# Six query weight blocks of 120 rows in place of five of 128, and another opening, in a one-core attention and gated-MLP kernel

## The chip, the cores and the metric

The kernel runs on one core of a Trainium2 chip. A core has five engines with queues of their own: TensorE (PE in the profile, with its weight loads as PEld), VectorE (DVE), ScalarE (ACT), GpSimd (POOL) and SyncE (SP), which here only issues DMA transfers. TensorE reads SBUF and writes PSUM (eight banks of 512 fp32 columns by 128 partitions), from which DVE or ACT copy results back to SBUF. The metric is the device time of one execution in microseconds, as the median of several runs.

## The reference

All tensors are bf16. With S = 2048 rows of x, width D = 640, H = 32 heads of 20 columns and F = 1536:

```python
xn = layernorm(x)                              # over the 640 columns, no scale or bias
q, k, v = split(xn @ wqkv)                     # wqkv: 640 x 1920, 32 heads of 20
pq, pk = q_h @ w_phi[h], k_h @ w_phi[h]        # w_phi: 32 matrices of 20 x 20
phi_q = [softmax(pq), softmax(-pq)]            # 40 features a head
phi_k = [softmax(pk), softmax(-pk)]
kv, z = sum_s phi_k^T v, sum_s phi_k           # linear attention, not causal
o   = (phi_q @ kv) / (phi_q . z + 1e-6)
out = x + o @ wo + (silu(xn @ w1) * (xn @ w3)) @ w2
```

The head matrices w_phi act on the projected q and k. The kernel folds them into the weights: with a block diagonal of the 32 matrices, xn @ (Wq @ diag(w_phi)) gives pq at once, and the same for k.

## The kernel before, in words

The rows are handled as 16 tiles of 128 rows (t = 0 to 15), the width as DC = 5 chunks of 128 columns, the MLP as four blocks of 512 rows by 12 chunks of 128 of F.

The kernel does not write its instructions in order by hand. Each part of the work is a stream, a generator of steps (`norms`, `transposes`, `fold_k`, `attention`, `loads`, `mlps` and others, from line 735 on). A planner at the end of the function picks, again and again, the step that can start first by its own costs, and appends its instructions to the engines' lists; the dictionary `done` carries conditions between streams. The order on each engine, the bank of each product and the semaphores follow from that, once, when the kernel is built. All instructions pass through one helper, so the profile gives nearly all of them line 102 (line 114 for DMA issues), and groups are told apart by their tiles.

The opening (`first_loads` at line 414, `consts` at 434, `norms` at 735, `transposes` at 798):

- Tile 0 of x is loaded in two halves, one issued by SP and one by ACT. Then SP issues tile 1, tile 2, half of V's weights (`wv`), tile 3, the first third of w1 and w3 (`w_s` in the profile), w_phi (`phi_s`), K's weights transposed by the DMA (the second half of `wqkT`), x tiles 4 to 15 in three loads, and Q's weights transposed (the first half of `wqkT`). ACT issues the other half of `wv`.
- Tile 0's statistics are made on DVE (`bn_stats` of two halves, `bn_aggr`), with the power -1/2 on POOL and the normalisation on DVE (`ln_apply`). Tile 1's are made on ACT by two sums. Tiles 2 and 3 use DVE again; the two halves of their statistics are separate steps, and tile 2's second half waits until tile 0 has been transposed.
- TensorE multiplies zeros at first (`warm_up`), transposes tile 0 against an identity (five transposes), multiplies zeros eight times more (`IDLE2`, written `PS<-t 128x128`), and then the V products of tile 0 start (`PS<-wv,xnT`), once the transposed tile has been copied from PSUM to `xnT`. `PARTS` at line 516 says in which pieces and by which engine: tile 0 in two, three chunks on ACT and two on DVE.
- The four tiles' V products, two MLP groups and four folds of K's weights come next, then the K and V products of the 16 tiles in turn (`Wkp` and `wv`). Tiles 4 to 15 are normalised on ACT or DVE and transposed by DMAs on SP (`xnT<-x_tok`, DMA_TRANSPOSE).

The folds (`block_diag` at 528, `fold_mm` at 536): `BDc` holds the block diagonal by chunks of 128 rows. Since 128 is no multiple of 20, the chunks share heads: each touches seven heads (140 columns) or eight (160 columns, split in two products of 80 at the bank's border). So a fold of one chunk of 128 input rows is six products, of 140, 140, 80, 80, 140 and 140 columns, all of 128 rows. K's five folds run early; Q's five stand behind tiles 9 to 13 in `attention`, one each, and are copied to `Wqp` by ACT or DVE.

Later stages: the sums over all tiles (`kv_sum`), then per tile the Q projection (`Wqp`), exponentials on ACT, sums and ratios on DVE and POOL, a DMA transpose (`eqT<-eq`), the token product (`KVc,eqT`), and between them the MLP groups of ten products of 512 columns; last the output products.

Of the kernel before, what the change touches and what calls it, by code (L numbers as in the profile page):

```python
# [3 lines left out]
ACT = mybir.ActivationFunctionType  # L4
# [5 lines left out]
D = 640  # L10
H = 32
DH = 20
# [237 lines left out]
def bass_parallel_sum__linear_kernel_hedgehog__glu_gated_swiglu__prompt_kernel(  # L250
# [11 lines left out]
    bf = DT.bfloat16  # L262
    LAG = 4.0
    QLEAD = 2
    IDLE1, IDLE2 = 7, 8
    f32 = DT.float32
    P = _Program(nc)

# [18 lines left out]
    GM = new("GM", [128, DC, H], bf)  # L287
    phi_s = new("phi_s", [128, DC, DH], bf)
    BDc = new("BDc", [128, DC, 8 * DH], bf)
    bst = new("bst", [128, T, 12], f32)  # L290
    mv = new("mv", [128, T, 2], f32)
    rstd = new("rstd", [128, T, 2], f32)
# [25 lines left out]

    RE = region(T * 2 * D * 2 + 96)
    ekt = new("ekt", [128, T * 2 * D + 48], bf, RE)  # L320
    hT3 = new("hT3", [128, FC, 512], bf, RE)
    w2_s = new("w2_s", [128, FC, D], bf, RE + 12288)
    eq = [new(f"eq{i}", [128, NG * 128], bf, (RKV, RE + 27648)[i // 2] + 2816 * (i % 2)) for i in range(4)]
# [5 lines left out]
    oT = new("oT", [128, DC, S], bf, RV)  # L329

    RW = region(12800)
    wqkT = new("wqkT", [128, 2 * DC, D], bf, RW)
    KVc = new("KVc", [128, NG * 64], bf, RW)
    half = new("half", [128, 2, 660], f32, RW + 1408)
    Sq = new("Sq", [128, 4, 72], f32, RW + 6688)
# [55 lines left out]
    def memset(eng, o, v):  # L391
        P.op(eng, "memset", [o], [], (o, v), cost=0.15 + free(o) / 960)
# [8 lines left out]
    out_t = out.rearrange("b (t p) d -> p (b t) d", p=128)  # L401
    wqkv_t = A_wqkv.rearrange("(c p) n -> p c n", p=128)
    phi_t = A_w_phi.rearrange("h d f -> (h d) f").rearrange("(c p) f -> p c f", p=128)
    w1_t = B_w1.rearrange("(c p) f -> p c f", p=128)
    w3_t = B_w3.rearrange("(c p) f -> p c f", p=128)

# [4 lines left out]
    def load_x(a, b):  # L411
        P.dma("SP", x_tok[:, a:b, :], x_t[:, a:b, :])

    def first_loads():
        def half_wv(eng, a):
            P.dma(eng, wv[:, :, a:a + 320], wqkv_t[:, :, 2 * D + a:2 * D + a + 320])

        P.dma("SP", x_tok[:, 0, 0:320], x_t[:, 0, 0:320])
        P.dma("ACT", x_tok[:, 0, 320:D], x_t[:, 0, 320:D])
        load_x(1, 2)  # L420
        load_x(2, 3)
        half_wv("ACT", 0)
        half_wv("SP", 320)
        load_x(3, 4)
        w13(0, 512)
        P.dma("SP", phi_s[:], phi_t)
        P.dma("SP", wqkT[:, DC:2 * DC, :], A_wqkv[:, D:2 * D], True)
        load_x(4, 8)
        load_x(8, 12)
        load_x(12, 16)  # L430
        P.dma("SP", wqkT[:, 0:DC, :], A_wqkv[:, 0:D], True)


    def consts():
        memset("DVE", t1[:, 2, :], 0.0)
        memset("DVE", warm[:], 0.0)
        act(warm[:], warm[:], ACT.Exp)
        memset("POOL", ident[:], 0.0)
        select(ident[:], 0, [[-1, 128]], 1, ALU.not_equal, 1.0)
        memset("POOL", GM[:], 1.0)  # L440
        select(GM[:], 0, [[128, DC], [-DH, H]], 1, ALU.is_ge, 0.0)
        select(GM[:], DH, [[-128, DC], [DH, H]], -1, ALU.is_gt, 0.0)
        memset("POOL", mhalf[:], -0.5)
        memset("DVE", v_heads(v2[:].rearrange("p t n -> p (t n)"))[:, :, :, DH], 1.0)
        memset("POOL", M3[:, 0:3], 1.0)
        select(M3[:, 0:3], 0, [[-40, 3]], 1, ALU.is_ge, 0.0)
        select(M3[:, 0:3], 40, [[40, 3]], -1, ALU.is_gt, 0.0)
        memset("POOL", ekt[:, T * 2 * D:T * 2 * D + 48], 1.0)
# [61 lines left out]
    def idle(n, cols):  # L510
        z = t1[:, 2, :]
        for i in range(n):
            j = 7 - i if cols == 512 else 7
            mm(bank(j, cols), z[:, 0:128], z[:, 0:cols], True, True, cost=cols / 1200)

    PARTS = (((0, 0, 3, "ACT"), (1, 3, DC, "DVE")), ((0, 0, 3, "ACT"), (1, 3, DC, "ACT")),
             ((0, 0, 3, "ACT"), (1, 3, DC, "ACT")), ((0, 0, 2, "DVE"), (1, 2, DC, "ACT")))

    def xn_transpose(t, k):
# [13 lines left out]
               phi_s[:, c, :].unsqueeze(1).to_broadcast([128, n, DH]),  # L533
               GM[:, c, h0:h1 + 1].unsqueeze(2).to_broadcast([128, n, DH]), ALU.mult)

    def fold_mm(which, dc, k, eng=None):
        first = [True, True]
        for e in range(DC):
            h0, h1 = heads_of_chunk(e)
            lo, hi = DH * h0, DH * (h1 + 1)  # L540
            for q in range(2):
                a, b = max(lo, 320 * q), min(hi, 320 * q + 320)
                if a < b:
                    mm(bank(k + q, b - a, a - 320 * q), wqkT[:, which * DC + e, 128 * dc:128 * dc + 128],
                       BDc[:, e, a - lo:b - lo], first[q], e == DC - 1 or (q == 0 and e == 2), True)
                    first[q] = False
        dst = (Wqp, Wkp)[which]
        o = dst[:, dc, :].rearrange("p (b c) -> p b c", c=320)
        if eng:
            copy(eng, o, bank2(k, 320))  # L550
        else:
            evac(o, bank2(k, 320))
# [128 lines left out]
    def mlp(b, fc, k, cut=DC, dc=None):  # L681
        n = nmlp[0] % 3
        nmlp[0] += 1
        for w, kk in ((w1_s, k), (w3_s, k + 1)):
            for i in range(DC):
                if kk > k and i == cut:
                    held.add(k // 2)
                    fold_mm(1, dc, banks(2), "ACT")
# [44 lines left out]
    done = dict.fromkeys(("w", "ln", "t", "f", "k", "n", "kv", "v", "u", "qp", "qn", "qd", "q", "o", "h", "v0", "bd"), 0)  # L733

    def norms():
        yield lambda: (first_loads(), consts())
        yield lambda: act_sum(1, ACT.Copy, bst[:, 1, 0:1])
        yield lambda: (ln_half(0, 0), ln_half(0, 1), ln_rstd(0, 1))
        yield lambda: scalar_op(1, mv[:, 1, 0:1], bst[:, 1, 0:1], -1.0 / D, 0.0)
        yield lambda: act_sum(1, ACT.Square, mv[:, 1, 1:2], mv[:, 1, 0:1])  # L740
        yield lambda: ln_apply(0)
        done["ln"] = 1
        yield lambda: ln_half(2, 0)
        yield lambda: act_rstd(1)
        while done["t"] < 1:
            yield None
        yield lambda: ln_half(2, 1)
        yield lambda: ln_apply(1)
        done["ln"] = 2
        yield lambda: ln_rstd(2, 1)  # L750
        yield lambda: ln_half(3, 0)
        yield lambda: ln_apply(2)
        done["ln"] = 3
        yield lambda: (ln_half(3, 1), ln_rstd(3, 1))
        yield lambda: ln_apply(3)
        done["ln"] = 4
        yield block_diag
        done["bd"] = 1
        todo = []
        for t in range(4, T + 2, 2):  # L760
            if t == T or t > done["k"] + 8:
                for u in todo:
                    yield lambda u=u: ln_apply(u)
                    done["ln"] = u + 1
                todo = []
            if t == T:
                break
            while t > done["k"] + 8:
                yield None
            yield lambda t=t: ln_stats(t, 2)  # L770
            for u in todo:
                yield lambda u=u: ln_apply(u)
                done["ln"] = u + 1
            todo = [t, t + 1]

    def fold_k():
        while done["u"] < 2:
            yield None
        for dc in range(1, DC - 1):
            yield lambda dc=dc: fold_mm(1, dc, banks(2), "ACT")  # L780
        done["f"] = 1

    done["w"] = 4
# [8 lines left out]
    def transposed(t):  # L792
        while done["ln"] <= t:
            yield None
        yield lambda: xn_transpose(t, banks(2))
        done["t"] = t + 1

    def transposes():
# [7 lines left out]
    def loads():  # L806
        while done["t"] < 4:
            yield None
        for t in range(4, T):
            while done["ln"] <= t:  # L810
                yield None
            yield lambda t=t: P.dma("SP", xnT[:, :, t * 128:(t + 1) * 128], x_tok[:, t, :], True)
            done["t"] = t + 1
            if t == 7:
                yield lambda: w13(512, 1024)
                done["w"] = 8
        yield lambda: w13(1024, 1536)
        done["w"] = 12

    def attention():  # L820
# [20 lines left out]
        for t in range(T):  # L841
            while done["t"] <= t:
                yield None
            yield lambda t=t: k_tile(t, banks(2))
            done["k"] = t + 1
            if t >= 4:
                yield v(t)
            if 9 <= t < 14:
                yield lambda dc=t - 9: fold_mm(0, dc, banks(2))
        yield lambda: P.dma("SP", wo_s[:], A_wo.rearrange("(c p) d -> p c d", p=128))  # L850
        done["v"] = 1

# [189 lines left out]
```

## Time and profile before

| | us |
|---|---|
| median of 3 runs | 268.14 (268.13 to 268.24) |
| the profiled execution's own time | 268.08 |
| its span, first to last instruction | 266.4 |
| TensorE busy in the span | 262.2 (98%) |
| DVE, ACT, POOL busy | 168.7, 100.8, 100.7 |
| mean granted TensorE clock | 1.000 |

The page gives one profiled execution. Its parts are the engines' busy time, the span in 40 slices, the DMA queues, the chain of waits that ended last, the costliest groups of instructions and the DMA issues. The chain is followed back from the last instruction: 96% of it is TensorE, 2% the DMA of x. In timelines a row is a group of like instructions: start, length over all of them, engine, operation, tiles, count, and in brackets the idle time before it with what ended it. Matmul lengths overlap, so the spacing of starts tells the pace. A DMA is shown by its issue (`SPq`, `ACTq`); its landing stands in the DMA view, as time from the issue.

### The profile page before, as it was taken

The page shows a single profiled execution, that of the slowest core. Times are in us where ns is not written, and L with a number is a line of the kernel's source. Part 1 is how long each engine was busy: PE and PEld are TensorE (multiplying, and loading weights), DVE is VectorE, ACT ScalarE, POOL GpSimd, SP SyncE. Part 2 cuts the span into 40 slices and gives each one's busy share as a digit, 9 for nine tenths or more (in the row PEclk, how much of TensorE's full clock was granted, in tenths as well). Part 3 has the DMA queues.
Part 4 walks back from the last instruction along what each step waited for, and adds up shares of the span by engine and source line. Part 5 has one row for each costly group of instructions (what it writes and reads, how often), then busy time and mean ns, then how long its engine had stood idle before and what let it go on. Part 6 is the DMA issues. An engine that isn't in the chain of part 4 may idle for free.

```text
span 266.4 us, 4813 instructions
## 1 busy us (share of the span) xinstructions
PE 262.2 (98%) x1959; PEld 159.4 (60%) x1959; DVE 168.7 (63%) x290; ACT 100.8 (38%) x199; POOL 100.7 (38%) x143
## 2 busy tenths in 40 slices
PE   7999999999999999999999999999999999999996
PEld 3656777777655555555554445544577777777773
DVE  4559998998766898888889877888511121212112
ACT  5667999887326334434433343322100000000000
POOL 4404896999984444455534334420000000000000
PEclk9999999999999999999999999999999999999999
DMA  7998792850393244454444444213212212131201
GB/s 211 304 320 159 145 218 53 186 190 2 100 282 75 55 92 92 86 97 81 79 81 79 80 81 79 51 35 75 49 52 75 74 59 91 52 98 49 90 36 49
DMA packets 63510, 27.73 MB, mean 104 GB/s; under 512 B 49920, under 2 KB 63488, under 8 KB 63488
## 3 DMA queue, kind: packets, MB, share of 16 engines
q1 hardware_dynamic: 62544, 26.90, 43.0%
q10 hardware_dynamic: 944, 0.52, 0.7%
q8 instruction: 15, 0.25, 0.4%
q14 instruction: 7, 0.06, 0.1%
HBM read 12.81 MB, written 2.62 MB: 58 GB/s over the span
## 4 chain that ended last, share of the span: by engine, by line
PE 96%; DMA 2%; DVE 1%; SPq 0%; POOL 0%; issue 0%
PE PS L102 96%; DMA x_tok<-in_A_x_dram 2%; SPq L114 0%; POOL rstd L102 0%; DVE bst L102 0%; DVE x_tok L102 0%; DVE xres L102 0%; DVE rstd L102 0%
## 5 line engine op out<-in xcount | busy, mean ns | idle before, releaser
L102 PE MATMUL PS<-xnT,w_s 128*128 128x512 bf16 x480 | 107.4, 379 | 0.0
L102 PEld LDWEIGHTS PS<-xnT,w_s 128*128 128x128 bf16 x480 | 45.9, 98 | 51.3
L102 PE MATMUL PS<-w_s,hT 128*128 128x320 bf16 (+2 forms) x384 | 54.9, 299 | 0.0
L102 DVE TENSOR_TENSOR xres<-PS,xres 128x640 bf16<-128x640 f32 (+2 forms) x17 | 13.4, 785 | 59.8 <-PE PS L102 59.8
L102 ACT ACTIVATE th<-PS 128x512 f32<-128x512 f32 x48 | 29.1, 605 | 48.0 <-PE PS L102 48.0
L102 PEld LDWEIGHTS PS<-w_s,hT 128*128 128x128 bf16 x384 | 37.1, 98 | 15.1
L102 DVE SCALAR_TENSOR_TENSOR t<-th,PS 128x512 bf16<-128x512 f32 x48 | 32.5, 677 | 20.2 <-ACT th L102 19.3
L102 POOL TENSOR_TENSOR ekt<-ekt,rS 128x640 bf16<-128x640 bf16 x32 | 39.6, 1277 | 2.6 <-DVE rS L102 2.6
L102 DVE SCALAR_TENSOR_TENSOR hT<-t,PS 128x512 bf16<-128x512 bf16 x48 | 33.0, 688 | 5.0
L102 ACT ACTIVATE eq<-PS 128x600 bf16<-128x600 f32 (+1 forms) x72 | 23.9, 418 | 32.0 <-PE PS L102 32.0
L102 PE MATMUL PS<-wo_s,oT 128*128 128x320 bf16 (+2 forms) x160 | 24.5, 299 | 0.0
L102 PE MATMUL PS<-wv,xnT 128*128 128x320 bf16 x160 | 24.4, 299 | 0.1
L102 PE MATMUL PS<-Wqp,xnT 128*128 128x512 bf16 (+1 forms) x160 | 24.3, 299 | 0.0
L102 PE MATMUL PS<-Wkp,xnT 128*128 128x320 bf16 x160 | 23.7, 299 | 0.0
L102 POOL TENSOR_TENSOR eq<-eq,rq 128x600 bf16<-128x600 bf16 (+1 forms) x32 | 22.7, 729 | 1.3
L102 POOL TENSOR_TENSOR rq<-rq,Sq 128x32 f32<-128x32 f32 x16 | 4.1, 255 | 50.1 <-DVE rq L102 50.1
L102 DVE TENSOR_REDUCE S<-ekt 128x64 f32<-128x1280 bf16 x16 | 22.9, 1431 | 0.0
L102 POOL TENSOR_TENSOR half<-eq 128x660 f32<-128x660 bf16 x15 | 20.4, 1358 | 4.5 <-ACT eq L102 4.5
L102 ACT ACTIVATE ekt<-PS 128x640 bf16<-128x640 f32 x32 | 20.9, 733 | 2.5 <-PE PS L102 2.5
L102 PEld LDWEIGHTS PS<-wo_s,oT 128*128 128x128 bf16 x160 | 15.5, 98 | 6.5
L102 PEld LDWEIGHTS PS<-wv,xnT 128*128 128x128 bf16 x160 | 15.4, 98 | 6.1 <-ACT xnT L102 0.2
L102 PEld LDWEIGHTS PS<-Wkp,xnT 128*128 128x128 bf16 x160 | 15.5, 98 | 5.9
(56 smaller groups left out, 178.3 us busy)
## 6 DMA issues: line engine op xcount, KB each, us to landing
w_s<-in_B_w_dram SPq DMA_DIRECT2D x6, 640.0 KB, 6.4
xres<-in_A_x_dram SPq DMA_DIRECT2D x16, 160.0 KB, 2.3
out_dram<-xres SPq DMA_DIRECT2D x15, 160.0 KB, 1.8
x_tok<-in_A_x_dram SPq DMA_DIRECT2D x3, 640.0 KB, 6.4
w_s<-in_B_w_dram SPq DMA_DIRECT2D x1, 1920.0 KB, 9.4
wo_s<-in_A_wo_dram SPq DMA_DIRECT2D x1, 800.0 KB, 7.2
x_tok<-in_A_x_dram SPq DMA_DIRECT2D x3, 160.0 KB, 4.0
wv<-in_A_wqkv_dram ACTq DMA_DIRECT2D x1, 400.0 KB, 4.0
```

What stands on the lines that cost most here:

```text
L102: o = _Op(eng, lambda: m(*args, **kw), r, w, cost)
```

## The change

Loads: tile 1 becomes ACT's first transfer, and both halves of tile 0 go out on SP, the second as SP's second issue. K's transposed weights have a tile of their own (`wkT`), placed in memory that is used later for `ekt`. Q's weights come as six blocks: block g holds the 128 columns from 120g on, transposed, of which 120 rows (six whole heads) are used; the last has 40. Three blocks are loaded where the one load stood, three behind tile 11's transposes. w_phi is loaded a second time in blocks of 120 rows (`phi_6`, two DMAs behind K's weights).

Fold: `BD6`, 120 rows by 6 blocks of 120 columns, is built on POOL by one multiplication with a mask `GM6` (three operations on POOL in `consts`), after the first MLP group. A fold of Q (`fold_q`) is five products of 120 columns and one of 40, on contiguous PSUM columns from 32 on, copied in one piece. K's fold keeps its form.

Opening: tile 0 is copied in three pieces, all on ACT (two, two and one chunk), each in a PSUM bank of its own. The zero products behind its transposes are five, not eight. The halves of tile 2's and 3's statistics are one step each; tile 2's no longer waits for tile 0's transposes and stands ahead of tile 1's normalisation on DVE. The memset of ones in v moves from DVE's start to behind the transposes of tile 3.

What follows from the planner, seen in the order of each engine: tile 3's transposes stand three products later; tile 3's V products come behind the first MLP group (ten products) instead of ahead of it. Between there and the Q projections the order is the same but for the folds. In the later stages, Q tiles 4 to 9 come in pairs (projection, MLP group, projection, token product, two groups, token product, group) where they came singly before; the numbers of products of each kind are the same.

```diff
-    IDLE1, IDLE2 = 7, 8
+    IDLE1, IDLE2 = 7, 5
...
+    GM6 = new("GM6", [128, 6], bf)
+    phi_6 = new("phi_6", [128, 6, DH], bf)
...
+    wkT = new("wkT", [128, DC, D], bf, RE + 20480)
...
-    wqkT = new("wqkT", [128, 2 * DC, D], bf, RW)
+    wqT = new("wqT", [128, 6, D], bf, RW)
+    BD6 = new("BD6", [128, 6, 120], bf, RW + 7680)
...
+        memset("POOL", phi_6[:, 5, :], 0.0)
         P.dma("SP", x_tok[:, 0, 0:320], x_t[:, 0, 0:320])
-        P.dma("ACT", x_tok[:, 0, 320:D], x_t[:, 0, 320:D])
-        load_x(1, 2)
+        P.dma("ACT", x_tok[:, 1, :], x_t[:, 1, :])
+        P.dma("SP", x_tok[:, 0, 320:D], x_t[:, 0, 320:D])
         load_x(2, 3)
...
-        P.dma("SP", wqkT[:, DC:2 * DC, :], A_wqkv[:, D:2 * D], True)
+        P.dma("SP", wkT[:], A_wqkv[:, D:2 * D], True)
+        P.dma("SP", phi_6[0:120, 0:5, :], phi_r[0:600, :].rearrange("(c p) f -> p c f", p=120))
+        P.dma("SP", phi_6[0:40, 5, :], phi_r[600:D, :])
         load_x(4, 8)
         load_x(8, 12)
         load_x(12, 16)
-        P.dma("SP", wqkT[:, 0:DC, :], A_wqkv[:, 0:D], True)
+        load_wqT(0, 3)
+
+    def load_wqT(a, b):
+        for g in range(a, b):
+            P.dma("SP", wqT[:, g, :], A_wqkv[:, 120 * g:120 * g + 128], True)
...
-        memset("DVE", v_heads(v2[:].rearrange("p t n -> p (t n)"))[:, :, :, DH], 1.0)
+        memset("POOL", GM6[:], 1.0)
+        select(GM6[:], 0, [[-DH, 6]], 1, ALU.is_ge, 0.0)
+        select(GM6[:], DH, [[DH, 6]], -1, ALU.is_gt, 0.0)
...
-    PARTS = (((0, 0, 3, "ACT"), (1, 3, DC, "DVE")), ((0, 0, 3, "ACT"), (1, 3, DC, "ACT")),
+    PARTS = (((0, 0, 2, "ACT"), (1, 2, 4, "ACT"), (2, 4, DC, "ACT")), ((0, 0, 3, "ACT"), (1, 3, DC, "ACT")),
...
+    def block_diag6():
+        o = BD6[0:120].rearrange("p c (h f) -> p c h f", f=DH)
+        tt("POOL", o, phi_6[0:120].unsqueeze(2).to_broadcast([120, 6, 6, DH]),
+           GM6[0:120].unsqueeze(1).unsqueeze(3).to_broadcast([120, 6, 6, DH]), ALU.mult)
+
+    def fold_q(dc, k):
+        c0 = k * 512 + 32
+        for g in range(6):
+            n = 120 if g < 5 else 40
+            mm(PS[:, c0 + 120 * g:c0 + 120 * g + n], wqT[0:120, g, 128 * dc:128 * dc + 128],
+               BD6[0:120, g, 0:n], g in (0, 4), g in (3, 5), True)
+        evac(Wqp[:, dc, :], PS[:, c0:c0 + D])
...
-        yield lambda: ln_half(2, 0)
         yield lambda: act_rstd(1)
-        while done["t"] < 1:
-            yield None
-        yield lambda: ln_half(2, 1)
+        yield lambda: (ln_half(2, 0), ln_half(2, 1))
         yield lambda: ln_apply(1)
...
-        yield lambda: ln_half(3, 0)
         yield lambda: ln_apply(2)
         done["ln"] = 3
-        yield lambda: (ln_half(3, 1), ln_rstd(3, 1))
+        yield lambda: (ln_half(3, 0), ln_half(3, 1), ln_rstd(3, 1))
         yield lambda: ln_apply(3)
         done["ln"] = 4
+        while done["t"] < 4:
+            yield None
+        yield lambda: memset("DVE", v_heads(v2[:].rearrange("p t n -> p (t n)"))[:, :, :, DH], 1.0)
         yield block_diag
         done["bd"] = 1
+        while done["u"] < 1:
+            yield None
+        yield block_diag6
...
-        yield lambda: xn_transpose(t, banks(2))
+        yield lambda: xn_transpose(t, banks(2 if t else 4))
...
+            if t == 11:
+                yield lambda: load_wqT(3, 6)
+                done["wq"] = 1
...
             if 9 <= t < 14:
-                yield lambda dc=t - 9: fold_mm(0, dc, banks(2))
+                while not done["wq"]:
+                    yield None
+                yield lambda dc=t - 9: fold_q(dc, banks(2))
```

More of the change, by code (lines that the diff above doesn't have):

```diff
@@ L403, in bass_parallel_sum__linear_kernel_hedgehog__glu_gated_swiglu__prompt_kernel @@
     phi_t = A_w_phi.rearrange("h d f -> (h d) f").rearrange("(c p) f -> p c f", p=128)
+    phi_r = A_w_phi.rearrange("h d f -> (h d) f")
     w1_t = B_w1.rearrange("(c p) f -> p c f", p=128)
@@ L534, in block_diag, with fold_mm @@
                GM[:, c, h0:h1 + 1].unsqueeze(2).to_broadcast([128, n, DH]), ALU.mult)
-    def fold_mm(which, dc, k, eng=None):
+    def block_diag6():
[9 more added lines that the diff above has]
+        evac(Wqp[:, dc, :], PS[:, c0:c0 + D])
+    def fold_mm(dc, k, eng=None):
         first = [True, True]
@@ L543, in fold_mm @@
                 if a < b:
-                    mm(bank(k + q, b - a, a - 320 * q), wqkT[:, which * DC + e, 128 * dc:128 * dc + 128],
+                    mm(bank(k + q, b - a, a - 320 * q), wkT[:, e, 128 * dc:128 * dc + 128],
                        BDc[:, e, a - lo:b - lo], first[q], e == DC - 1 or (q == 0 and e == 2), True)
                     first[q] = False
-        dst = (Wqp, Wkp)[which]
-        o = dst[:, dc, :].rearrange("p (b c) -> p b c", c=320)
+        o = Wkp[:, dc, :].rearrange("p (b c) -> p b c", c=320)
         if eng:
@@ L687, in mlp @@
                     held.add(k // 2)
-                    fold_mm(1, dc, banks(2), "ACT")
+                    fold_mm(dc, banks(2), "ACT")
                     held.discard(k // 2)
@@ L731, in banks @@
         return min((k for k in range(0, 8, n) if k // 2 not in held), key=free_at)
-    done = dict.fromkeys(("w", "ln", "t", "f", "k", "n", "kv", "v", "u", "qp", "qn", "qd", "q", "o", "h", "v0", "bd"), 0)
+    done = dict.fromkeys(("w", "ln", "t", "f", "k", "n", "kv", "v", "u", "qp", "qn", "qd", "q", "o", "h", "v0", "bd", "wq"), 0)
     def norms():
@@ L779, in fold_k @@
         for dc in range(1, DC - 1):
-            yield lambda dc=dc: fold_mm(1, dc, banks(2), "ACT")
+            yield lambda dc=dc: fold_mm(dc, banks(2), "ACT")
         done["f"] = 1
```

## The prediction

> **What bounds the kernel now.** I read the page first, then the chain of waits, then the busy time by stage, then the opening as a timeline. The first row is the page's part 1; the others are stages, each with its length, then busy time of PE, its weight loads, DVE, ACT and POOL; then the longest piece of the chain.
>
> ```profile
> PE 262.2 (98%) x1959; PEld 159.4 (60%) x1959; DVE 168.7 (63%) x290; ACT 100.8 (38%) x199; POOL 100.7 (38%) x143
> ...
> 7.56:13.25 5.69, 5.69 (x50) 4.07 (x51) 2.66 (x9) 4.09 (x8) 2.37 (x6) 1.00 1.21 299
> 13.25:62.00 48.75, 48.75 (x375) 33.70 (x373) 44.03 (x74) 42.28 (x66) 34.56 (x47) 1.00 0.76 174
> 62.00:184.00 122.00, 122.00 (x935) 63.66 (x933) 99.10 (x168) 48.99 (x116) 60.51 (x76) 1.00 0.42 87
> ```
>
> ```profile
> 7.56 256.48 PE PS L102 x1926
> ```
>
> From 7.56 us, where TensorE transposes tile 1, the chain is TensorE alone, and each stage has it busy for its whole length. So the change pays in two places only: what starts that run earlier, and TensorE time removed from it. Anything that makes it wait is a loss in full.
>
> The opening, from the timeline (start, length, engine, operation):
>
> ```profile
> 0.80 0.41 ACTq L114 DMA_DIRECT2D x_tok<-in_A_x_dram  x1
> 0.81 1.34 SPq L114 DMA_DIRECT2D x_tok<-in_A_x_dram  x3
> ...
> 3.07 0.50 DVE L102 MEMSET v<- 128x528 bf16 x1 [1.85 <-issue]
> ...
> 3.19 0.82 DVE L102 BATCH_NORM_STATS2 bst<-x_tok 128x6 f32<-128x320 bf16 x2
> ...
> 4.22 0.74 ACT L102 ACTIVATE t<-x_tok 128x640 bf16<-128x640 bf16 x1 [0.99 <-DMA x_tok<-in_A_x_dram]
> ...
> 4.54 0.57 POOL L102 TENSOR_TENSOR rstd<-rstd,mhalf 128x1 f32<-128x1 f32 x1 [1.28 <-DVE rstd L102]
> ...
> 5.16 0.44 DVE L102 TENSOR_SCALAR x_tok<-x_tok,mv,rstd 128x640 bf16<-128x640 bf16 x1
> ...
> 5.65 0.45 PE L102 MATMUL PS<-ident,x_tok 128*128 128x128 bf16 x5 [0.38 <-DVE x_tok L102]
> ...
> 5.94 0.61 PE L102 MATMUL PS<-t 128*128 128x128 bf16 x8
> ...
> 6.10 0.47 ACT L102 ACTIVATE xnT<-PS 128x384 bf16<-128x384 bf16 x1
> ...
> 6.63 0.85 PE L102 MATMUL PS<-wv,xnT 128*128 128x320 bf16 x5
> ...
> 7.94 0.77 ACT L102 ACTIVATE xnT<-PS 128x384 bf16<-128x384 bf16 x2 [1.37 <-PE PS L102]
> ...
> 10.92 0.45 PE L102 MATMUL PS<-ident,x_tok 128*128 128x128 bf16 x5
> ...
> 11.21 2.20 PE L102 MATMUL PS<-wv,xnT 128*128 128x320 bf16 x15
> 11.25 0.29 DVE L102 COPY xnT<-PS 128x256 bf16<-128x256 bf16 x1 [0.38 <-PE PS L102]
> ...
> 13.25 4.05 PE L102 MATMUL PS<-xnT,w_s 128*128 128x512 bf16 x18
> ```
>
> Tile 0's statistics end at 4.01; call this E. Its transposes start 1.64 later (5.65), its first product after 0.98 more (6.63), and tile 1's transposes at 7.56, which is E+3.55. The eight idle products fill TensorE while tile 0 is copied; products follow each other at 0.136 (fifteen between 11.21 and 13.25), so the five of 6.63 have issued by 7.31 and TensorE then waits 0.25 for tile 1, whose sum on ACT began only at 4.22.
>
> **The change part by part.** *Loads of tiles 0 and 1.* Landing times, from the DMA view of short stretches (last number: us from issue):
>
> ```profile
> x_tok<-in_A_x_dram SPq DMA_DIRECT2D x1, 160.0 KB, 2.9
> x_tok<-in_A_x_dram ACTq DMA_DIRECT2D x1, 80.0 KB, 2.5
> x_tok<-in_A_x_dram SPq DMA_DIRECT2D x1, 80.0 KB, 2.3
> ```
>
> Tile 0's halves land at 3.1 and 3.3, tile 1 (SP's second issue, 1.26) at 4.2. Afterwards tile 1 goes out at 0.80 on ACT, tile 0's second half as SP's second issue, about 0.81+0.41 = 1.22. Its landing L is not in the trace. Early bound: the quickest half, 1.22+2.3 = 3.5. Late bound: now 240 KB stand ahead of it, and with it 320 KB, as many as had to land when tile 1 did at 4.2. I take 3.75, nearer the early row, since it is half a tile, issued like that row and beside a tile whose transfer starts at 0.80. Statistics of one half take 0.47, so E = 3.75+0.02+0.47 = 4.24, 0.23 later than now.
>
> [...]
>
> *Three copies, five idle products.* Tile 3's first copy starts 0.33 after its transposes. A 256-column copy on ACT takes about 0.38 (the pair of 384 and 256 columns takes 0.77, the first alone 0.47, with some overlap), so tile 0's first product starts 0.33+0.38+0.05 = 0.76 after its transposes instead of 0.98. The other two copies follow about 0.28 apart and hold the third and fifth product by hundredths: five products end 1.45 after the transposes, at E+1.64+1.45 = E+3.09. The idle products end 0.57 after, before the copy. DVE: tile 1's rstd follows tile 0's apply (E+1.6), then both halves of tile 2's statistics (0.86) and tile 1's apply at E+2.45, so tile 1 is ready at E+2.95. TensorE is the later one, and the 0.25 wait goes. Tile 1's transposes: 4.24+3.09 = 7.33, that is -0.23 (between -0.48 for L=3.5 and +0.22 for L=4.2).
>
> *From there on* the same 35 products and 15 transposes follow. Tile 3's last ten products move behind the first MLP group, which needs tile 3's copy: transposes +0.33+0.29+0.05 = 0.67 against 0.56 of cover (five transposes, two products), a new wait of 0.1; today's gaps in this stretch (5.69 against 35x0.136+15x0.058 = 5.63) are worth 0.06 and go. Net +0.05.
>
> ```profile
> w_s<-in_B_w_dram SPq DMA_DIRECT2D x1, 640.0 KB, 6.5
> ...
> wqkT<-in_A_wqkv_dram SPq DMA_TRANSPOSE x1, 10.3
> ...
> 11.97 1.97 POOL L102 TENSOR_TENSOR BDc<-phi_s,GM 128x140 bf16<-128x140 bf16 x5 [1.59 <-DMA phi_s<-in_A_w_phi_dram]
> ...
> 14.28 7.76 SPq L114 DMA_TRANSPOSE wqkT<-in_A_wqkv_dram  x1
> ...
> 17.14 0.48 PE L102 MATMUL PS<-BDc,wqkT 128*128 128x140 bf16 x6
> ...
> 20.71 0.23 POOL L102 TENSOR_SCALAR rstd<-mv 128x2 f32<-128x2 f32 x1 [6.76 <-DVE mv L102]
> ...
> 23.46 6.96 PE L102 MATMUL PS<-Wkp,xnT 128*128 128x320 bf16 x50
> ```
>
> The MLP's first weights land at 3.23+6.5 = 9.7, needed near 11.8. K's transposed weights land at 5.86+10.3 = 16.2, needed at 16.9: 0.7 of cover.
>
> *Hidden edits.* The 0.50 memset of v leaves DVE's start for a place behind tile 3's copy, where DVE has nothing to do until the first MLP group's gate: 0; without that cover 0.5. POOL's four small operations (some 0.6) fit into its 1.28 idle before tile 0's power: 0. The second block diagonal has 720 columns like the first, about 2.0, inside POOL's 6.76 idle ahead of 20.71: 0. The two small phi loads stand on SP behind K's weights and ahead of tiles 4 to 15; at worst they delay these by some 2. Tile 4 is the first of them; its statistics are done when POOL takes them at 20.71, and TensorE multiplies it as the fifth of the tiles from 23.46 on, at 23.46+40x0.136 = 28.9: 8 us of cover, 0.
>
> *The query fold.*
>
> ```profile
> 45.19 0.48 PE L102 MATMUL PS<-BDc,wqkT 128*128 128x140 bf16 x6
> 45.51 0.71 PE L102 MATMUL PS<-Wkp,xnT 128*128 128x320 bf16 x4
> ...
> L102 PEld LDWEIGHTS PS<-BDc,wqkT x60: 97/98/99, 16.9 to 57.5; 128*128 128x128 bf16 x60
> ...
> 36.12 2.75 SPq L114 DMA_TRANSPOSE xnT<-x_tok  x2
> ...
> 43.45 2.52 SPq L114 DMA_TRANSPOSE xnT<-x_tok  x2
> ...
> xnT<-x_tok SPq DMA_TRANSPOSE x1, 2.6
> ```
>
> A fold takes 0.32 now (45.19 to 45.51) for 720 columns in six products; afterwards 640 columns in six: 0.32x640/720 = 0.29, so -0.03 each and -0.13 for five; the other end is 0 if the count sets the time. Its weights come in six loads instead of one, about 1.26 of SP each (2.52 for two). The last three stand behind tile 11's transposes, which end at 38.87, and ahead of tile 12's (43.45): 38.9+2x1.28 = 41.5 for the last, landed 2.6 later at 44.1, against 45.19. Cover 1.1; 0.
>
> *The order behind 85 us.* Query tiles now come in pairs. A token product stands 16.3 behind its projection before and 15.5 after in the first of a pair.
>
> ```profile
> 108.74 1.40 SPq L114 DMA_TRANSPOSE eqT<-eq  x1
> ...
> eqT<-eq SPq DMA_TRANSPOSE x1, 4.5
> ...
> 115.14 0.48 PE L102 MATMUL PS<-KVc,eqT 128*128 128x63 bf16 x11
> ```
>
> The operand lands at 113.2 for a product at 115.1: 1.9 of cover, of which 0.8 goes. I take 0; the other end is below.
>
> **Sum.** -0.23+0.05-0.13 = -0.31 on the profiled execution's 268.08, that is 267.77; the median of the runs (268.14) stands 0.06 above it, so 267.8.
>
> **The rivals.** *Tile 0 is not held up* (L at 3.5 or less): -0.48+0.05-0.13 = -0.56, or 267.5. For it: the quickest half's 2.3. Against: 160 KB issued ahead on ACT; and what is late next is tile 2, whose statistics now stand ahead of tile 1's apply, so it has to land earlier too. *No gain* (L at 4.2, the late bound): +0.22+0.05-0.13, 268.3. *Late query weights, slower:* the blocks start 240 bytes apart. If a load of a block takes twice its 1.28 on SP, the last lands at 38.9+7.6+1.3 = 47.8, and the first query fold holds TensorE for 2.6: 270.4. It decides from 1.28+0.37 = 1.65 a load on. Against: tile transposes of the same size keep to 1.26. [...] *Narrow products lose their hidden weight load, slower:* 6x0.098 = 0.59 a fold instead of 0.32, +1.35 for five instead of -0.13: 269.3. No product in the trace has under 128 rows, so nothing excludes it. *Pairs, slower:* if two MLP evacuations on DVE (1.4) come ahead of a tile's sums, 1.1 of cover falls short by 0.3 in each of four pairs: 1.2, or 269.0.
>
> **How the numbers follow.** The forecast (L between 3.5 and 4.2, its other terms good to 0.15) has 0.54, on 267.4 to 268.2 around 267.8. A run can tell some 0.2%, 0.54 us, from no change: a quarter of the forecast, 0.13, lies below 267.6, and 0.41 within. Tile 0 not held up 0.18 (faster), no gain 0.03 (within), late weights 0.08, narrow products 0.07, pairs 0.10 (all slower). So faster 0.31, within 0.44, slower 0.25. The range takes in the forecast, the early case and the pairs, and leaves out the other two slow ones: 267.3 to 269.0.
>
> **What would show it.** Right: tile 0's statistics end at 4.1 to 4.3, tile 1's transposes start at 7.2 to 7.4 with no wait of TensorE ahead, a fold spans 0.29, and no DMA releases TensorE at the first query fold. Wrong: statistics ending after 4.5, a fold over 0.45, TensorE idle near 45, or token products that wait on eqT.

## The result, and the profile after

The changed kernel takes 268.74 us (median of 11 runs, 267.97 to 269.76) beside 268.24 (11 runs, 268.07 to 268.44) for the kernel before: a ratio of 1.0024 [1.0016, 1.0031], so 0.64 us slower by the ratio, 0.50 by the two medians. The forecast was 0.31 faster. Its runs spread over 1.8 us where those of before spread over 0.4. Twelve more runs later on (e8 below) gave 268.27 beside 268.18, 1.0007 [0.9996, 1.0018]: the loss there is smaller and not clear of no change. The profiled execution took 268.74, its span is 267.0 (before 268.08 and 266.4).

The engines' busy time from the page's part 1 and, of the chain of waits, the pieces around its only break:

```profile
PE 262.4 (98%) x1956; PEld 159.4 (60%) x1956; DVE 168.4 (63%) x289; ACT 101.5 (38%) x201; POOL 102.5 (38%) x148
...
6.81 101.55 PE PS L102 x865
...
113.83 1.42 POOL eq L102 x2
115.28 5.63 DMA eqT<-eq
120.95 143.72 PE PS L102 x984
```

Before, one piece of TensorE ran from 7.56 to the end. Now it is broken once: the second long piece starts at 120.95, released by a DMA transpose of eq that took 5.63. Up to there the kernel is ahead, as the stages by time show (length, busy time of PE, its weight loads, DVE, ACT, POOL). After:

```profile
7.51:23.43 15.92, 15.92 (x123) 9.61 (x121) 9.65 (x25) 10.56 (x19) 6.21 (x14) 1.00 1.09 269
23.43:62.91 39.48, 39.48 (x311) 28.82 (x310) 37.56 (x58) 36.84 (x57) 32.54 (x41) 1.00 0.75 154
62.91:120.20 57.29, 57.29 (x514) 31.31 (x511) 46.16 (x77) 24.45 (x63) 35.74 (x42) 1.00 0.48 102
120.20:184.00 63.80, 63.19 (x409) 31.21 (x407) 51.80 (x91) 23.75 (x52) 24.27 (x34) 1.00 0.40 76
```

and the same two first stages before:

```profile
7.56:23.46 15.90, 15.90 (x121) 9.56 (x121) 9.97 (x27) 10.57 (x19) 5.33 (x13) 1.00 1.15 296
23.46:63.07 39.61, 39.61 (x312) 28.97 (x311) 37.79 (x57) 36.87 (x57) 32.67 (x41) 1.00 0.64 139
```

The borders are the same points of the work: tile 1's transposes, the first K product, the first Q projection. The opening has gained 0.03 (23.43 for 23.46), the stage with the folds 0.13 (39.48 for 39.61), together 0.16 at 63 us. In the last stage shown TensorE is busy 63.19 of 63.80, the one stage with idle time. There it is, in the timeline of TensorE after:

```profile
118.82 1.52 PE L102 MATMUL PS<-Wqp,xnT 128*128 128x512 bf16 x10
120.95 0.49 PE L102 MATMUL PS<-KVc,eqT 128*128 128x63 bf16 x11 [0.61 <-DMA eqT<-eq]
```

The ten products of a projection and the token product of tile 6 behind them. In the kernels below without this wait, the token product starts 1.36 behind the start of the projection; here it would be 118.82+1.36 = 120.18, so the wait costs 0.77. With it, -0.16 has become +0.63 at the token product of the last tile (183.80 for 183.17), and +0.66 at the end of the profiled execution.

Why did this transpose take 5.63? The DMA view of 118 to 121 us (busy share of the engines, then packets, MB and share of 16 engines' time by queue, then what was issued):

```profile
DMA  9979999999999900000000000000001000000990
...
q1 hardware_dynamic: 876, 0.21, 111.6%
...
q8 instruction: 1, 0.02, 3.5%
...
oT<-o_tok SPq DMA_TRANSPOSE x1, 4.8
```

Beside the kernel's own queue there is one packet on a queue called "instruction", 0.02 MB, that took 3.5% of 16x3 = 1.68 us, from 118.24 on; it is called an instruction load below. In the packets of the trace, 19 of the transposes' 256-byte pieces that start from 118.75 on took about 2 us instead of 18 ns, up to 120.8; the operand of tile 6 landed at 120.91. The trace doesn't name a packet's engine, so that these pieces stood on the engine that the load held is inferred. The transpose of `o_tok` in the same stretch was late as well (4.8). Such packets return every 17 to 21 us in this part of both kernels (after at 101.3, 118.2, 138.5; before at 102.1, 119.9, 137.8), and before the change one hit too:

```profile
q8 instruction: 1, 0.02, 1.3%
...
oT<-o_tok SPq DMA_TRANSPOSE x1, 4.2
```

This transpose, of another tile (`oT`), usually lands 2.6 after its issue. There it was late by 1.6 and nothing waited for it.

In the trace's packets this one is 16,384 bytes, like the other 14 of its queue (on the page of the changed kernel: q8, 15 packets, 0.25 MB). A second instruction queue (q14: 7 packets, 0.06 MB) has packets of 8,192 bytes. What the packets hold, and how an engine chooses between the queues, no trace shows; the 2 us is what this trace measured.

### The profile page after: what moved, and what is told of

Read it like the earlier page. It is cut to its first block, busy times and chain, and to the rows that moved or that the text cites. A ratio compares the mean times of both kernels' runs of the same rounds, so it can differ in the third digit from the quotient of the medians.

```text
span 267.0 us, 4825 instructions
## 1 busy us (share of the span) xinstructions
PE 262.4 (98%) x1956; PEld 159.4 (60%) x1956; DVE 168.4 (63%) x289; ACT 101.5 (38%) x201; POOL 102.5 (38%) x148
## 3 DMA queue, kind: packets, MB, share of 16 engines
HBM read 12.83 MB, written 2.62 MB: 58 GB/s over the span
## 4 chain that ended last, share of the span: by engine, by line
PE 92%; DMA 3%; DVE 2%; POOL 1%; ACT 1%; issue 0%; DVEq 0%
PE PS L102 92%; DMA eqT<-eq 2%; DMA x_tok<-in_A_x_dram 1%; ACT eq L102 1%; POOL eq L102 1%; DVE bst L102 0%; DVE Sq L102 0%; DVE t L102 0%; DVE hT L102 0%; POOL rstd L102 0%; ACT th L102 0%; DVE x_tok L102 0%; DVE rq L102 0%; DVE xres L102 0%; DVE mv L102 0%
## 5 line engine op out<-in xcount | busy, mean ns | idle before, releaser
L102 PEld LDWEIGHTS PS<-Wqp,xnT 128*128 128x128 bf16 x160 | 13.2, 98 | 11.6
```

What stands on the lines that cost most here:

```text
L102: o = _Op(eng, lambda: m(*args, **kw), r, w, cost)
```

## The experiments

Two theories stood after this result. A: the pairs of Q tiles left a transpose little room, and an instruction load that fell on it made TensorE wait; neither alone does harm. B: the pairs (or another part of the change) cost time by themselves. The zero products at the start (`idle`) serve as the lever on the loads: each is a product and a weight load, two instructions, and none takes part in the result. If a load comes once TensorE has used up a certain number of instructions, more zero products bring it forward.

**e1: single tiles again.** The whole change, with the planner held to single Q tiles from tile 4 on:

```diff
-            while t > done["qn"] + 1 or t > done["u"] / 3 + QLEAD or t >= 2 and not done["kv"]:
+            while t > done["qn"] + 1 or t > done["u"] / 3 + QLEAD or t >= 2 and not done["kv"] or t >= 4 and t > done["q"] + 2:
```

> The changed kernel with one condition more for the Q projections: tile t from 4 on waits until the token product of tile t-3 stands, which restores the order of single tiles. Theory 1 (the loss is one token product that waits for its transposed operand, because pairs leave it 1.1 to 1.6 us of cover): no TensorE wait on eqT, 267.9 to 268.1 against 268.24 of before, and runs within 0.4 us of each other as with the kernel before (the changed kernel: within 1.8). Theory 2 (opening, fold or the new places in memory cost it): 268.7, and the spread stays.

Measured: 267.94 (267.82 to 268.21) beside 268.07, 0.9996 [0.9987, 1.0004]. All transposes of eq land 3.5 to 3.9 after their issue, and none is waited for. Loads come at 100.6, 119.6 and 137.7. The order is near the former one, not the same: tile 3's token product still stands 3.8 behind tile 2's, as in the pairs (6.0 before), while tile 6 has 6.35 from its transpose's issue to its product, near the 6.38 of before. The folds and the opening of the change are in this trace and the wait is not; that fits a loss that belongs to the pairs. By the medians alone it is not shown, since the changed kernel wasn't timed beside this run, and in e8 it lost only 0.09. And the loads have moved with the order, so this run doesn't separate A from B.

**e2: the loads earlier.** The changed kernel with 27 more zero products, narrower, so that their time stays the same: `idle(34, 26)` for `idle(7, 128)`, 54 instructions more.

> The changed kernel, pairs kept, with the seven zero products of 128 columns at the very start written as 34 of 26 columns: the same TensorE time while it waits for x, but 27 products (54 instructions) more, so each 16 KB load of TensorE's instructions comes some 5 to 6 us earlier: the one of 118.2 us at 112.4, when no transpose is under way. Theory 1a (the operand is late because that load blocks the DMA that the transpose needs): the wait of 0.8 us at 120 goes, 267.9 to 268.2. Theory 1b (the transpose is late for another reason, such as the two transposes issued back to back in a pair): the wait stays, 268.6 to 268.8.

Measured: 268.45 (268.10 to 268.90) beside the same 268.07, 1.0011 [1.0002, 1.0020]. The load of 118.2 came at 113.7, 4.5 earlier (112.4 was expected), and the transpose of tile 6 landed on time. But the next came at 134.6 instead of 138.5, onto the transpose of another tile. DMA view of e2, the transposes of eq issued at 115.1 and at 131.95, and the load's row for 134 to 137.1:

```profile
eqT<-eq SPq DMA_TRANSPOSE x1, 3.6
...
eqT<-eq SPq DMA_TRANSPOSE x1, 5.0
...
q8 instruction: 1, 0.02, 1.8%
```

and its timeline of TensorE there:

```profile
135.29 1.52 PE L102 MATMUL PS<-Wqp,xnT 128*128 128x512 bf16 x10
136.95 0.49 PE L102 MATMUL PS<-KVc,eqT 128*128 128x63 bf16 x11
```

135.29+1.36 = 136.65, so this token product is 0.30 late. The wait went with the load, from tile 6 to a tile 17 us further on. The profiled execution, with its wait of 0.30, was the quickest of the eleven (268.10); the median is 0.35 above that, which this trace doesn't account for.

**e5: the loads later.** `idle(2, 448)`: five zero products, ten instructions, fewer.

> The changed kernel, pairs kept, with the seven zero products at the start written as two of 448 columns: five products (ten instructions) fewer, so each 16 KB load of TensorE's instructions comes about 1.1 us later: 102.4, 119.3 and 139.6 instead of 101.3, 118.2 and 138.5, just behind the landing of a pair's transpose each time. Theory 1a (such a load blocks the transpose that is under way, and pairs leave too little cover): no wait on eqT, 267.9 to 268.1. Theory 1b (pairs are late for a reason of their own): 268.5 to 268.8 as in the changed kernel and the run with the loads 5 us earlier.

Measured: 267.96 (267.76 to 268.48) beside 268.11, 0.9995 [0.9986, 1.0004]. The load came at 119.7, 1.5 later. Its neighbours did not follow: they came at 100.7 and 137.7, a little earlier than in the changed kernel, where 102.4 and 139.6 were expected. In e5, the transpose of eq issued at 115.1, then the load's row for 119.2 to 121:

```profile
eqT<-eq SPq DMA_TRANSPOSE x1, 3.6
...
q8 instruction: 1, 0.02, 3.5%
```

and TensorE:

```profile
118.67 1.52 PE L102 MATMUL PS<-Wqp,xnT 128*128 128x512 bf16 x10
120.03 0.48 PE L102 MATMUL PS<-KVc,eqT 128*128 128x63 bf16 x11
```

The transpose had landed at 118.7, ahead of the load. The token product starts 1.36 behind the projection, with no wait; the pairs are as in the changed kernel, and TensorE waits for no transpose in this trace. So the pairs by themselves cost nothing, and B falls as far as it laid the cost on the order alone.

**e6: single tiles, with a load on the transpose.** e1 with `idle(17, 52)`, 20 instructions more, which bring its load back to where it fell in the changed kernel.

> The kernel with Q tiles single again, with the zero products written as 17 of 52 columns: 20 instructions more, so the loads come about 2.2 us earlier, at 98.4, 117.4 and 135.5, inside the time in which a transpose of eq is under way (96.1 to 99.6, 114.6 to 118.1, 132.5 to 136.0). Theory 1a with cover as the deciding size: eqT lands 1 to 2 us late in one or more of these, and TensorE still does not wait, since single tiles leave 2.8 us or more: 267.9 to 268.1. If any late transpose costs time whatever the order, 268.4 or more.

Measured: 268.04 (267.80 to 268.70) beside 268.11, 0.9997 [0.9988, 1.0006]. In e6, the transpose issued at 115.0 and the load's row for 118 to 121:

```profile
eqT<-eq SPq DMA_TRANSPOSE x1, 5.2
...
q8 instruction: 1, 0.02, 1.8%
```

and TensorE:

```profile
121.34 0.48 PE L102 MATMUL PS<-KVc,eqT 128*128 128x63 bf16 x11
```

The load came at 118.1 (117.4 was expected) and the transpose landed at 120.2, 5.2 behind its issue (5.6 in the changed kernel, 5.3 in e8), but the token product was due only at 121.34, and TensorE didn't wait. With the 4.9 that the pairs leave from issue to product (115.10 to 120.03 in e5), the same landing would have been 0.3 late. e5 and e6 are the two crossed cases: in their traces, pairs without the collision and the collision without pairs both cost nothing. It takes both, which is A. The medians alone can't tell the two from the changed kernel in e8 below: the intervals overlap.

**e8: the changed kernel again, and e9: its loads 20 instructions earlier** (`idle(17, 52)`), on one chip.

> The changed kernel once more, beside the next run on one chip. If its loss is the wait found at 120 us: 268.5 to 268.8, some 0.5 above the kernel before, with runs up to 1.5 us apart.

> The counterpart, with pairs kept, to the run that puts the loads of instructions 2.2 us earlier under single tiles (17 zero products of 52 columns, 20 instructions more): loads near 99, 116 and 136.3. The transpose issued at 115.1 is under way from 116 to 118.7 and the one issued at 132.0 from 133 to 135.5, so the first is met near its start, the second is landed. If cover decides, this costs a wait at the token product near 120 where the single order with the same loads cost none: 268.3 to 268.8.

Measured: e8 268.27 (267.71 to 269.23), e9 268.19 (267.82 to 268.79), beside 268.18; ratios 1.0007 [0.9996, 1.0018] and 1.0002 [0.9993, 1.0010]. In e8 the load at 118.4 made the transpose issued at 115.44 land after 5.3, and the token product was due at 119.01+1.36 = 120.37:

```profile
119.01 1.52 PE L102 MATMUL PS<-Wqp,xnT 128*128 128x512 bf16 x10
120.76 0.49 PE L102 MATMUL PS<-KVc,eqT 128*128 128x63 bf16 x11 [0.23 <-DMA eqT<-eq]
```

0.39 late: the same wait at the same place in another execution, of half the size. In e9 the load came at 117.1 and the transpose issued at 115.22 landed after 4.6:

```profile
118.79 1.52 PE L102 MATMUL PS<-Wqp,xnT 128*128 128x512 bf16 x10
120.15 0.48 PE L102 MATMUL PS<-KVc,eqT 128*128 128x63 bf16 x11
```

115.22+4.6 = 119.8, just covered, so no wait. I had expected a longer delay and a wait in e9, and that missed: how long a transpose is held up differs (1.1 in e9, 1.8 in e8, 2.1 in the first profile, over its usual 3.5), between two executions of the same kernel and with the point at which the load meets it (1.9 behind its issue in e9, 2.9 in e8). This fits the spread: the runs of the changed kernel reach over 1.8 and 1.5 us, those of e1 and e5 over 0.4 and 0.7, and the quickest run of the changed kernel, 267.71, is as quick as theirs (267.82, 267.76). It fits, and over the five traces with pairs the profiled time rises with the wait (no wait 267.81 and 267.96, 0.30 268.10, 0.39 268.54, 0.77 268.74). But the median of e9, whose trace has no wait, isn't told apart from e8's, and of each built kernel only one execution has a trace.

**e3 and e4: the two halves of the change alone.** Both with single Q tiles (the condition of e1). e3 keeps the fold and undoes the opening; its core, against e1:

```diff
-    IDLE1, IDLE2 = 7, 5
+    IDLE1, IDLE2 = 7, 8
...
-        P.dma("ACT", x_tok[:, 1, :], x_t[:, 1, :])
-        P.dma("SP", x_tok[:, 0, 320:D], x_t[:, 0, 320:D])
+        P.dma("ACT", x_tok[:, 0, 320:D], x_t[:, 0, 320:D])
+        load_x(1, 2)
...
```

e4 keeps the opening and undoes the fold; its core, against the kernel before:

```diff
-        P.dma("ACT", x_tok[:, 0, 320:D], x_t[:, 0, 320:D])
-        load_x(1, 2)
+        P.dma("ACT", x_tok[:, 1, :], x_t[:, 1, :])
+        P.dma("SP", x_tok[:, 0, 320:D], x_t[:, 0, 320:D])
...
-    PARTS = (((0, 0, 3, "ACT"), (1, 3, DC, "DVE")), ((0, 0, 3, "ACT"), (1, 3, DC, "ACT")),
+    PARTS = (((0, 0, 2, "ACT"), (1, 2, 4, "ACT"), (2, 4, DC, "ACT")), ((0, 0, 3, "ACT"), (1, 3, DC, "ACT")),
...
```

> The query fold of the change alone (loads, order and copies of the opening as before), with the condition that keeps Q tiles single. Theory 1: five folds at 0.29 instead of 0.32 us, 0.13 faster than before: 268.1. If the six loads or the products of 120 rows cost something, 268.3 or more.

> The opening of the change alone (fold as before), with the condition that keeps Q tiles single. By the trace of the changed kernel, where K products start 0.03 earlier: 268.2, a gain of 0.0 to 0.1. The prediction's own term was -0.18, which would be 268.06.

Measured: e3 267.91 (267.80 to 270.40; one run of eleven at 270.40, with a granted clock of 0.994 beside 1.000, widens the interval), 1.0003 [0.9985, 1.0020]; e4 268.03 (267.93 to 268.25), 0.9997 [0.9988, 1.0005]. By the medians, beside 268.07, -0.16 for the fold and -0.04 for the opening; with both, in e1, -0.13. None of these is clear of no change, but the folds are plain in the traces: 0.29 each in e3 and 0.32 in e4, and in the first pair of traces -0.13 for their stage. The opening's -0.03 is smaller than the differences between executions (below).

**e7: the loads of tiles 0 and 1 as before,** the rest of the opening new (against e1):

```diff
-            P.dma("ACT", x_tok[:, 1, :], x_t[:, 1, :])
-            P.dma("SP", x_tok[:, 0, 320:D], x_t[:, 0, 320:D])
+            P.dma("ACT", x_tok[:, 0, 320:D], x_t[:, 0, 320:D])
+            load_x(1, 2)
```

> The kernel with Q tiles single, and the loads of tiles 0 and 1 as before the change (tile 0 in halves on SP and ACT, tile 1 second on SP); the three copies, the five zero products and the order on DVE stay. Tile 0's statistics should end at 4.0 instead of 4.4 and its first product start near 6.45; tile 1's sum then starts at 4.2 again, and its transposes at 7.4 to 7.6 instead of 7.5. Theory A (the loads move as much as they cost): 267.9 to 268.0, no difference from the same kernel with the changed loads. Theory B (holding up tile 0 is what ate the opening's gain): 267.6 to 267.8.

Measured: 267.88 (267.70 to 268.35) beside 268.11, 0.9994 [0.9985, 1.0002]; e5, the changed kernel without its wait, had 267.96 on the same chip. Its DVE, the statistics of tile 2:

```profile
6.32 0.89 DVE L102 BATCH_NORM_STATS2 bst<-x_tok 128x6 f32<-128x320 bf16 x2 [0.31 <-DMA x_tok<-in_A_x_dram]
```

and TensorE, the transposes of tiles 0 and 1:

```profile
5.64 0.45 PE L102 MATMUL PS<-ident,x_tok 128*128 128x128 bf16 x5
...
7.60 0.45 PE L102 MATMUL PS<-ident,x_tok 128*128 128x128 bf16 x5
```

Tile 0's statistics end at 4.02 as before the change, 0.35 earlier than in it, and its transposes start at 5.64. But tile 2 now lands at 6.3, and tile 1's normalisation stands behind tile 2's statistics on DVE: tile 1's transposes start at 7.60 (7.51 in the changed kernel), after a wait of 0.26. In this pair of traces the new loads move the wait from tile 1 to tile 0 and gain 0.09. But the late tile 2 need not be the loads' doing: with the same loads it landed at 5.75 before the change and at 5.69 in e3. And by the medians e7 is, if anything, the quicker one. So whether the new loads gain or lose is not shown, and theory B is not excluded.

## Why the prediction was wrong, point by point

**The step that failed** is "The order behind 85 us": "1.9 of cover, of which 0.8 goes. I take 0". Cover is the time from an operand's landing to its use. The place was right, and the 0.8 is right for what it counts: after, tile 6's token product would stand 16.87 behind the start of its projection (120.18 less 103.31), before it stood at 17.67. But cover also hangs on when the transpose is issued, and that I left as it was. Tile 6 before, the issue of its transpose and its token product:

```profile
114.75 1.38 SPq L114 DMA_TRANSPOSE eqT<-eq  x1
...
121.13 0.48 PE L102 MATMUL PS<-KVc,eqT 128*128 128x63 bf16 x11
```

That is 6.38 from issue to use. After, the issue is at 115.28 and the product due at 120.18: 4.90, and 4.7 for tiles 3, 5 and 9. So 1.5 of cover went, not 0.8. The other 0.7 is the issue, which stands 11.96 behind the projection instead of 11.28. DVE shows why; the sums of tile 6 are `Sq`, first before, then after:

```profile
110.91 0.84 DVE L102 TENSOR_TENSOR o_tok<-PS,den_s 128x660 bf16<-128x660 f32 x1
111.67 0.83 DVE L102 TENSOR_REDUCE Sq<-half 128x66 f32<-128x660 f32 x1
```

```profile
110.42 0.69 DVE L102 SCALAR_TENSOR_TENSOR t<-th,PS 128x512 bf16<-128x512 f32 x1 [0.24 <-ACT th L102]
111.59 0.69 DVE L102 SCALAR_TENSOR_TENSOR hT<-t,PS 128x512 bf16<-128x512 bf16 x1 [0.48 <-DVE t L102]
112.20 0.83 DVE L102 TENSOR_REDUCE Sq<-half 128x66 f32<-128x660 f32 x1
```

Before, the sums follow the division of another tile (`o_tok`) at once; after, the two steps by which DVE evacuates an MLP group (`t`, `hT`) come between.

The second fault is that I took one row, 4.5, for the landing time, as if it were a fixed number. It was the one late landing of 16 before (the others 3.5 to 3.7), and in its stretch, 108.7 to 113.3, the DMA view has a packet of a second queue of that kind:

```profile
q14 instruction: 1, 0.01, 0.4%
...
eqT<-eq SPq DMA_TRANSPOSE x1, 4.5
```

After, with 4.90 from issue to use, a transpose that lands in its usual 3.5 is 1.4 ahead of its product, one that takes 4.5 is still 0.4 ahead, and the one of tile 6 took 5.63: late by 120.95-120.18 = 0.77. Had only 0.8 gone, as said, that same landing would have cost less than 0.1. So the price of 0 was right without a collision and also with the landing that I had read; the two faults together made the 0.77. That 1.9-0.8 = 1.1 lies near the 1.4 measured is chance, since the 1.1 was counted from a late landing and the 1.4 from a usual one.

Over all eleven traces of this document, 19 of 176 transposes of eq take longer than 3.7 to land, and each of the 19 has an instruction packet in its stretch. Of the other 157, 30 have one too, all but three of these at the very start or end of the stretch. So in these traces no landing is late without a packet under way, but a packet doesn't always make one late. TensorE waited for three of the 19: tile 6 in the changed kernel and in e8, and the one in e2. The spread stood in the trace of before: oT came 1.6 late there, and 1.6 on the usual 3.5 is more than 4.90. No end of my range was read from it. That the range (267.3 to 269.0) holds the measured 268.74 is luck: its upper end is the price of four waits that didn't come.

**The rival "Pairs, slower"** gave the right waiter, token products in pairs, and 269.0. Its condition came true in the rows above: two MLP evacuations on DVE (0.69 each) stand right ahead of tile 6's sums. But they take 0.7 of cover and by themselves make no wait: e5 has the same order, its transpose issued 11.93 behind the projection, and none. In the changed kernel's traces there is one wait, of 0.77 and 0.39, where the delay of the DMA comes on top. The four waits of 0.3 are refuted; the mechanism was half of the true one, and the order step should have counted it.

**Loads, E and the opening.** DMA view and DVE of the changed kernel (tile 1 and the first half of tile 0, issued at 0.81; the second half, at 1.26):

```profile
x_tok<-in_A_x_dram ACTq DMA_DIRECT2D x1, 160.0 KB, 2.8
x_tok<-in_A_x_dram SPq DMA_DIRECT2D x1, 80.0 KB, 2.6
...
x_tok<-in_A_x_dram SPq DMA_DIRECT2D x2, 80.0 KB, 2.6
```

```profile
3.45 0.92 DVE L102 BATCH_NORM_STATS2 bst<-x_tok 128x6 f32<-128x320 bf16 x2 [2.24 <-DMA x_tok<-in_A_x_dram]
```

The second half landed at 3.85, near the 3.75 taken and not at the late bound of 4.2. But the first, which I had left at 3.1, came at 3.4: beside a whole tile it takes 2.6 (2.45 to 2.62 in the eight traces with these loads), beside another half it took 2.3 (three traces). DVE began there and the two halves ran on to E = 4.37, not 4.24. The rest, from TensorE after:

```profile
6.00 0.51 PE L102 MATMUL PS<-ident,x_tok 128*128 128x128 bf16 x5 [0.40 <-DVE rstd L102]
...
6.81 0.86 PE L102 MATMUL PS<-wv,xnT 128*128 128x320 bf16 x5
7.51 0.44 PE L102 MATMUL PS<-ident,x_tok 128*128 128x128 bf16 x5
...
11.47 0.43 PE L102 MATMUL PS<-wv,xnT 128*128 128x320 bf16 x2
11.85 2.33 PE L102 MATMUL PS<-xnT,w_s 128*128 128x512 bf16 x10
```

Tile 0's transposes start at E+1.63 (1.64 said), the first product 0.81 after them (0.76 said), tile 1's transposes at E+3.14 (3.09 said) without a wait. The steps held; the start was 0.13 later than said and the copies 0.05. Tile 1's transposes therefore stand at 7.51, not 7.33, and the term is -0.05 instead of -0.23. Ahead of the first MLP group TensorE waits 11.85-(11.47+2x0.136) = 0.11 (0.1 said), and the stretch to 23.43 is 0.02 longer (0.05 said). The opening as a whole: -0.03 measured in this execution, -0.18 said. Other executions with the same opening differ by more than that: tile 1's transposes start between 7.35 and 7.52 in its eight traces, and the first K product at 23.27 to 23.44 in six of them, at 23.62 in e8 and at 23.79 in e6, where TensorE waits 0.31 for `wv`; with the old opening it stands at 23.46 before and at 23.54 in e3. The mechanism holds; the term's size lies between the forecast and nothing, and these traces don't fix it.

**The fold.** Two rows of TensorE after, a fold and what follows it, and one of SP, the last three blocks of Q's weights:

```profile
45.16 0.45 PE L102 MATMUL PS<-BD,wqT 120*128 120x120 bf16 x6
45.45 0.84 PE L102 MATMUL PS<-Wkp,xnT 128*128 128x320 bf16 x5
```

```profile
38.70 3.90 SPq L114 DMA_TRANSPOSE wqT<-in_A_wqkv_dram  x3
```

0.29 a fold, as said, and -0.13 for the stage. The sum behind it has a slip that helped: 0.32x640/720 is 0.284, which would have made -0.18 for five. Products of 120 rows keep the pace of those of 128 closely enough (640 columns in 0.293, 720 in 0.315) to exclude the rival of the lost weight loads. Three blocks took 3.90 of SP, 1.30 each (1.28 said), and nothing waited at 45.16: the rival of late weights is excluded too, but with little to spare. No run shows a load of twice 1.28. The last block, issued at 41.33, landed later than the 2.6 taken:

```profile
wqT<-in_A_wqkv_dram SPq DMA_TRANSPOSE x1, 3.4
```

That is 44.7, 0.3 ahead of the fold's first weight load at 45.03, where 1.1 of cover was said. The issue is nearly the same (1.30 a block beside 1.26 for a tile). Whether the longer landing comes from the blocks' starts, 240 bytes apart, is open, since the blocks read DRAM, and the tile transposes that landed in 2.6 read SBUF.

**Hidden edits.** The memset, the small operations of POOL, the second block diagonal and the loads of w_phi cost nothing: in the two stages by time in which they lie TensorE is busy from end to end (15.92 of 15.92, 39.48 of 39.48).

Taken together: with the wait left out, the terms measure -0.16 in this execution for a forecast of -0.31, near the medians of e1 and e5 (-0.13 and -0.15, neither clear of no change); e5's own trace stands 0.30 ahead at the first Q projection (62.77 for 63.07). With the wait, the medians of its two sets of runs are a loss of 0.50 and of 0.09.

**What stays open.** Why one load takes 0.9 and another 1.7 us, and why the pieces behind it are late by up to 2 us in one execution and less in the next. In the changed kernel, e8 and e9 some 20 pieces each take over 1 us; in e2 and e6 none does, and the pieces only start late. And whether the slowest runs of the changed kernel (up to 269.76, 1.8 us above the quickest of their set) are this wait alone: none of them has a trace.

## What to carry to other kernels

Cover runs from the landing of a transfer to its use, so a change of order has to be counted at both ends: when the transfer is issued and when it is needed. One landing in a trace is not a fixed number: list all landings, those of like transfers too, and count the cover against the longest delay (before the change oT's 1.6, where eq's worst was 1.0). An edit in one place can shift the order and the instruction count for everything behind it, so a planner's change of order, or the place where instruction loads fall, has to be separated from the edit (here by holding the order, and by adding instructions that do nothing) before the edit is judged. One wait of 0.39 to 0.77 outweighed all that the other edits gained (0.13 and 0.15 by the medians of e1 and e5).

## What the runs showed of the hardware that was not expected

Instruction loads come in the middle of the work, beside the kernel's own transfers: one packet of 16 KB for 0.9 to 1.7 us, and transposes of eq that it met in e2, e6, e8, e9 and the changed kernel landed 1.1 to 2.1 us late. That such a packet holds one of the 16 DMA engines that carry the kernel's data is inferred from these delays. That these loads are TensorE's is read from the lever: only TensorE's instructions were added or taken away, and 54 more moved one load from 118.2 to 113.7, 20 more moved it forward by 1.1 to 1.5 and ten fewer back to 119.7, while the 8 KB packet of the other instruction queue stayed at 112.2 to 112.7. The lever is not exact: with ten fewer the next load came earlier (137.7 for 138.5), and with 20 more in e6 it came later than in e1 (138.1 for 137.7). Still, a few instructions at the start can decide which transfer is hit 110 us later.
